# Attention plus gated MLP on one core: the first 512 tokens in two pairs of tiles, the maxima written from ScalarE's DMA queue, output loads issued over three steps

## The chip, the core and the metric

The kernel runs on one core of one Trainium2 chip. A core has five engines with queues of their own: TensorE (PE, matmuls; PEld is its weight load), VectorE (DVE), ScalarE (ACT), GpSimd (POOL) and SyncE (SP, which here only issues DMAs). Matmul results go to PSUM, eight banks of 128 partitions x 512 floats; everything else lies in SBUF or, through DMAs, in device memory. The metric is device time in microseconds of one execution, the median over the runs.

## The reference

```python
# x: 2048 tokens x 512; 32 heads of 16; gMLP with 896 + 896 features
def _A_ref(x, wqkv, wo):                      # attention
    q, k, v = ...(x @ wqkv)...                # (B, H, S, 16) each
    p = softmax(einsum("bhqd,bhkd->bhqk", q, k) * 16 ** -0.5)
    return (p @ v).merged_heads @ wo
def _B_ref(x, w_in, w_sp, b_sp, w_out):       # mixer
    z = gelu(x @ w_in)
    z1, z2 = z[..., :896], layernorm(z[..., 896:])
    g = einsum("ts,bsf->btf", w_sp, z2) + b_sp[None, :, None]
    return (z1 * g) @ w_out

x = A_x
xn = layernorm(x)
return x + _A_ref(xn, A_wqkv, A_wo) + _B_ref(xn, B_w_in, B_w_sp, B_b_sp, B_w_out)
```

## The kernel before

**Precision.** Matmuls take operands of type fp32r. Where full precision is wanted an operand is kept as two parts, high and low: the high part is a copy into fp32r, the low part is the difference between the value and the high part. A product is then three matmuls into one PSUM bank: high by high, low by high, high by low (`mm3`, lines 161 to 164). `split` makes both parts from PSUM, the high one on ACT, the low one on DVE. The pair of buffers `hilo` exists three times.

**Layout.** 16 tiles of 128 tokens make 4 groups of 512. Heads come in 16 pairs `p`; m (0 to 3) counts blocks of 128 columns of Q or K, which serve four pairs each. The operands of a pair's scores lie in the stacks `qst` and `kst`, two of each, used in turn; they are written from scratch tensors in device memory (`qscr`, `kscr`) by `load_stacks`.

**Prologue** (from line 816 on). Everything is emitted in the order written by hand, and every engine runs its own instructions in that order. `load_x(g)` loads 4 token tiles in two DMAs of 512 KB; `norm_x` is the layer norm (statistics on DVE, scale and shift on ACT) in two parts of two tiles; it is a generator, and each `next` emits a further piece. `turn_x(g)` transposes a group, 16 transposes of 128x128 through PSUM, for one block of 128 features after the other, into `xnT`, split into high and low; one PSUM buffer of the tag `s`, of which there are three, serves each of the four blocks. Weights come by `begin` (DMA into a buffer for raw values and, in the prologue, a second DMA of the same values on POOL's queue straight into the high part) and `end` (low part, on DVE in the prologue; elsewhere POOL copies the high part and subtracts). Then for each group: `qk_group` makes Q and K of m = 0 (24 matmuls), `v_tile` four V tiles (12 matmuls each), and after two of these the next group is transposed. The four V weight blocks are parked in the second pair of stacks. Stores of `xnT` go by POOL's queue until the prologue ends.

**Main loop** (from line 947 on). It runs over halves of steps; a pair of halves handles three key tiles. `b` counts key tiles and begins below zero, since the row maxima run 27 steps (`LEAD`) ahead of the scores. In each half the maxima's matmuls (`max_mm`, tile `mx`, line 630), DVE's reduction (`max_red`, line 638), the scores (tile `st`, line 903), ACT's exponential (`exp`, into `pf`) and, in even halves, the product with V (`pv`, tile `o`, line 877) are emitted. `st` and `mx` share the three PSUM buffers of the tag `s`. PSUM banks d and o take the accumulators.

When the sixteenth step of a maximum group is reduced, `max_fin` forms the negated maxima of 512 queries in two parts, transposes them into `ms` (line 657), writes them to `mscr` and reads them back into two extra rows for each head of `qst`. `later(k, ...)` emits a DMA k halves later on SP's queue; here the write comes one half later and the four reads two halves later.

All other matmul work (the rest of Q and K, both MLP projections, the spatial product, the output products) are generators in `queue`, drawn in odd halves up to a credit in nanoseconds of PE. While b is below 0 the credit is 2600 in every half, even ones included; afterwards it comes from what is left to do. `mlp_out` makes the MLP's output tiles: for each it loads two pieces `hp` of the hidden product and the token tile `xr` one tile ahead, all three at once.

**The planner's estimates.** `gps(us)` adds a duration to `pool[0]`, an estimate of when POOL will have finished; `pool_done` lets a generator wait until the estimated clock has reached it. `load` holds estimates for ACT and DVE. These decide where instructions are put, not when they run.

Of the kernel before, what the change touches and what calls it, by code (L numbers as in the profile page):

```python
# [8 lines left out]
F32 = mybir.dt.float32  # L9
# [7 lines left out]
P = 128  # L17
# [22 lines left out]
def fused_block(ctx, tc, x, wqkv, wo, w_in, w_spT, b_sp, w_out, out):  # L40
# [59 lines left out]
    def move(dst, src):  # L100
        nc.sync.dma_start(raw(dst), raw(src))
# [23 lines left out]
    def later(k, fn, *args):  # L125
        late.append((now[0] + k, fn, args))

    def flush():
        due = [l for l in late if l[0] <= now[0]]
        late[:] = [l for l in late if l[0] > now[0]]  # L130
        for _, fn, args in due:
            fn(*args)
# [35 lines left out]
    def begin(nm, src, n, blocks=1, t=None, early=None):  # L168


        t = piece(nm) if t is None else t
        rw = t512(nm + "r") if early == "t" else big.tile([P, 512], F32, tag="raw", name=nm + "r", bufs=3)
        dst, hi = rw[:, :n], t[:, 0, :n]
        if blocks > 1:
            src = src.rearrange("(c p) f -> p c f", p=P)
            dst, hi = (v.rearrange("p (c f) -> p c f", c=blocks) for v in (dst, hi))
        move(dst, src)
        if early:
            nc.gpsimd.dma_start(hi, src)
        return t, rw, n  # L180

    def end(loaded, early=False):
        t, rw, n = loaded
        if early:
            nc.vector.tensor_sub(t[:, 1, :n], rw[:, :n], t[:, 0, :n].bitcast(F32))
        else:
            gps(0.6).tensor_copy(t[:, 0, :n], rw[:, :n])  # L187
            gps(1.3).tensor_sub(t[:, 1, :n], rw[:, :n], t[:, 0, :n].bitcast(F32))
        return t
# [33 lines left out]
    def load_x(g):  # L223
        xt = [at.tile([P, 2, D], F32, tag="pf", name=f"x{g}_{i}", bufs=PF) for i in (0, 2)]
        for i in range(len(xt)):
            k = 4 // len(xt)
            t = 4 * g + k * i
            rows = x[t * P:(t + k) * P, :]
            move(xt[i], rows if k == 1 else rows.rearrange("(a p) d -> p a d", p=P))
            for j in range(k):  # L230
                xs[g, k * i + j] = xt[i] if k == 1 else xt[i][:, j, :]

    def norm_x(g, parts=1):


        mv = sm.tile([P, 4, 2], F32, tag="mv", name=f"mv{g}", bufs=2)
        rs = sm.tile([P, 2, 4], F32, tag="rs", name=f"rs{g}", bufs=2)
        k = 4 // parts
        for a in range(parts):
            tiles = range(a * k, (a + 1) * k)  # L240
            sl = slice(a * k, (a + 1) * k)
            for i in tiles:
                st = sm.tile([P, 6], F32, tag="bst", name=f"bst{g}_{i}", bufs=4)
                nc.vector.bn_stats(st, xs[g, i])
                nc.vector.bn_aggr(mv[:, i, :], st)
            yield
            nc.scalar.activation(rs[:, 0, sl], mv[:, sl, 1], AF.Sqrt, bias=epst)
            nc.vector.reciprocal(rs[:, 0, sl], rs[:, 0, sl])
            nc.vector.scalar_tensor_tensor(rs[:, 1, sl], mv[:, sl, 0], -1.0, rs[:, 0, sl], ALU.mult, ALU.mult)
            for i in tiles:  # L250
                if i % 4 == 2:
                    yield
                nc.scalar.activation(xs[g, i], xs[g, i], AF.Identity, bias=rs[:, 1, i:i + 1], scale=rs[:, 0, i:i + 1])

    def turn_x(g):
        for c in range(ND):
            pt = spsum(f"xT{g}_{c}")[:, 0, :]
            for i in range(4):
                nc.tensor.transpose(pt[:, i * P:(i + 1) * P], xs[g, i][:, c * P:(c + 1) * P], ident)
            t = piece(f"xnT{g}_{c}")  # L260
            split(t[:, 0, :], t[:, 1, :], pt, 512)
            store(xscr[g][c], t)
            xnT[g, c] = t

    def fetch_xnT(g, k=0):

# [64 lines left out]
                yield from qk_group(m, g, [wq[m, a] for a in range(2)])  # L331


    def v_tile(t, ws):
        acc = dpsum(f"v{t}", "do"[t % 2])
        sl = slice((t % 4) * P, (t % 4 + 1) * P)
        for c in range(ND):
            xt = xnT[t // 4, c]
            mm3(acc, xt[:, 0, sl], xt[:, 1, sl], ws[c][:, 0, :], ws[c][:, 1, :], c == 0, c == ND - 1)
        act(vhead[:, t, :, :DH], acc.rearrange("p (h d) -> p h d", d=DH), AF.Copy, 512)  # L340
# [224 lines left out]
    def mlp_out():  # L565
        def load(t):
            hp = []
            for i, n in enumerate((4, 3)):
                h = piece(f"hp{t}_{i}")
                move(h[:, :, :n * P].rearrange("p a (f q) -> p a f q", q=P), hscr[t // 4][:, :, t % 4, 4 * i:4 * i + n, :])  # L570
                hp.append(h)
            xt = t512(f"xr{t}")
            move(xt, x[t * P:(t + 1) * P, :])
            return hp, xt

        nxt = load(0)
        yield -3
        for t in range(NT):
            hp, xt = nxt
            if t + 1 < NT:  # L580
                nxt = load(t + 1)
            if t == NT - 1:
# [12 lines left out]
            yield 0  # L595
# [14 lines left out]


    NSTEP = NP * 64
    mstep = {}
    mmax = {}

# [24 lines left out]
    def max_fin(i):  # L640
# [15 lines left out]
        ms = at.tile([P, 32], F32, tag="ms", name=f"ms{g}", bufs=2)  # L656
        nc.vector.transpose(ms, mrow.bitcast(F32))
        load["D"] += 0.6
        later(1, move, mscr[g % 4].rearrange("b k x -> (b k) x"), ms)
        for j in range(2):  # L660
            for a in range(2):
                row = 64 * j + KS + a
# [150 lines left out]

    engines = {mybir.EngineType.PE, mybir.EngineType.Activation, mybir.EngineType.DVE, mybir.EngineType.Pool, mybir.EngineType.SP}
    with tc.manual_schedule(engines=engines):
        load_x(0)
        w0 = [begin(*qk_weights(0, a), early="t") for a in range(2)]
        load_x(1)
        ones = big.tile([P, 512], F32, tag="raw", name="ones", bufs=3)
        nc.vector.memset(ones[0:32, 0:P], 1.0)  # L820
        wv = []
        for c in range(ND):
            t = (qst, kst)[c // 2][1].rearrange("p (b a f) -> p b a f", b=2, a=2)[:, c % 2]
            wv.append(begin(f"wv{c}", wqkv[c * P:(c + 1) * P, 2 * D:3 * D], 512, t=t, early="rt"[c % 2]))
        nc.gpsimd.dma_start(cscr.rearrange("o (a b) -> (o a) b", b=P), ones[0:16, 0:P])
        nc.gpsimd.memset(vhead[:, :, :, DH:], 1.0)
        nc.gpsimd.memset(vall[:, NT * H * (DH + 1):], 0.0)
        run(norm_x(0, 2))
        load_x(2)
        w0 = [end(l, True) for l in w0]  # L830
        turn_x(0)
        load_x(3)
        init_rows(0)
        wv = [end(l, True) for l in wv]
        norm = norm_x(1, 2)
        for g in range(NG):
            for y in qk_group(0, g, w0, ("d", "o")):
# [105 lines left out]
        for half in range(-2 * LEAD // 3, 2 * (N // 3 + 4)):  # L943
# [109 lines left out]
```

## Time and profile before

| | |
|---|---|
| median of 3 runs | 1964.72 us (1963.83 to 1965.18) |
| profiled execution | 1965.23 us, of which the span of the trace 1963.1 us |
| mean granted TensorE clock | 0.997 |
| DMA | 294.20 MB, mean 150 GB/s |
| SP's DMA queue waiting for `ms` of DVE | 210.8 us in 58 waits |
| SP's DMA queue waiting for the landing of `mscr` | 81.1 us in 48 waits |

The page gives, for each engine, its busy time and share of the span; PE's ends are modelled, so a busy PE is not necessarily PE at its peak rate. The costliest groups of instructions follow, with the mean of one and the idle time of the engine before them:

```profile
L638 DVE TENSOR_REDUCE mm<-mx 128x2 f32<-128x1024 f32 x1024 | 1221.5, 1222 | 501.3 <-PE mx L630 497.2
L57 ACT ACTIVATE pf<-st 128x1024 f32<-128x1024 f32 x1024 | 1028.7, 1025 | 621.9 <-PE st L903 597.2
L877 PE MATMUL o<-pf,vall 128*32 128x512 f32 (+1 forms) x5120 | 511.0, 513 | 0.0
```

In a line of the timeline the first number is the start in us from the start of the span, the second how long the merged instructions took from first start to last end, then engine, line, operation, output and inputs, shape and count; in brackets stands how long the engine had been idle before it and who released it. Line 57 is a helper through which most of ACT's work goes, line 101 the helper of SP's DMAs, so such lines are told apart by their tiles.

### The profile page before, as it was taken

Reading aid. Unit: us, or ns where it says so; the run is one execution under the profiler, and the core shown is the slowest. Engines: PE = TensorE matmul, PEld = TensorE weight load, DVE = VectorE, ACT = ScalarE, POOL = GpSimd, SP = SyncE. Lnnn points to the kernel's source line nnn. Section 1 sums busy time; section 2 is a strip of 40 time slices with the busy share of each in tenths; the row PEclk is TensorE's granted clock in tenths of the full one; section 3 lists DMA queues with packets and bytes.
Section 4 is the critical chain, followed back from the end, with each engine's and each line's share of the span. In section 5 each row is a group of like instructions: output and inputs, shape, how many; then the busy total and the mean of one; then the engine's idle time right before and its main releaser. Section 6 shows DMA issues by size and latency. Waiting matters only on the chain.

```text
span 1963.1 us, 32545 instructions
## 1 busy us (share of the span) xinstructions
PE 1933.9 (99%) x12544; PEld 1047.0 (53%) x12544; DVE 1372.9 (70%) x1562; ACT 1231.7 (63%) x1402; POOL 720.9 (37%) x787
## 2 busy tenths in 40 slices
PE   7999999999999999999999999999999999999998
PEld 6765555555555555555555555555555555555543
DVE  5256777777777677777777777777777777777872
ACT  4336778888777665656666665665566655556664
POOL 2234368789776931026122531017112300002100
PEclk9999999999999999999999999999999999999999
DMA  9586444363535645365545744346364645355323
GB/s 327 204 292 200 139 107 122 108 176 111 154 117 159 187 123 140 91 162 159 151 138 154 211 129 125 108 126 204 105 163 135 176 142 145 106 152 154 105 73 113
DMA packets 234195, 294.20 MB, mean 150 GB/s; under 512 B 34536, under 2 KB 134520, under 8 KB 231160
## 3 DMA queue, kind: packets, MB, share of 16 engines
q1 hardware_dynamic: 229816, 282.08, 49.4%
q0 software_dynamic: 4224, 10.04, 1.4%
q8 instruction: 99, 1.62, 0.3%
q14 instruction: 56, 0.46, 0.1%
HBM read 190.09 MB, written 101.97 MB: 149 GB/s over the span
## 4 chain that ended last, share of the span: by engine, by line
PE 91%; DVE 3%; POOL 2%; DMA 2%; ACT 1%; issue 1%; SPq 0%; DVEq 0%; POOLq 0%; ACTq 0%
PE o L877 23%; PE mx L630 15%; PE st L903 15%; PE sp L162 7%; PE sp L164 5%; PE sp L163 5%; PE mo L162 2%; PE z1p L162 2%; PE qk L162 1%; DVE mm L638 1%; PE mo L163 1%; PE mo L164 1%; PE z2p L162 1%; PE z1p L164 1%; PE z1p L163 1%; PE qk L163 1%
## 5 line engine op out<-in xcount | busy, mean ns | idle before, releaser
L638 DVE TENSOR_REDUCE mm<-mx 128x2 f32<-128x1024 f32 x1024 | 1221.5, 1222 | 501.3 <-PE mx L630 497.2
L57 ACT ACTIVATE pf<-st 128x1024 f32<-128x1024 f32 x1024 | 1028.7, 1025 | 621.9 <-PE st L903 597.2
L877 PE MATMUL o<-pf,vall 128*32 128x512 f32 (+1 forms) x5120 | 511.0, 513 | 0.0
L630 PE MATMUL mx<-kst,qst 48*128 48x512 f32 x2048 | 446.9, 434 | 3.1 <-DVE mm L638 2.0
L903 PE MATMUL st<-qst,kst 50*128 50x512 f32 x2048 | 445.6, 432 | 1.5 <-DVE mm L638 1.4
L630 PEld LDWEIGHTS mx<-kst,qst 48*128 48x128 f32 x2048 | 192.0, 185 | 268.7 <-ACT pf L57 168.6
L903 PEld LDWEIGHTS st<-qst,kst 50*128 50x128 f32 x2048 | 193.3, 185 | 164.0 <-issue 85.7
L877 PEld LDWEIGHTS o<-pf,vall 128*32 128x32 f32 x5120 | 131.4, 109 | 233.7 <-issue 211.7
L162 PE MATMUL sp<-wsp,zs 128*128 128x512 f32 x448 | 193.8, 433 | 0.3 <-DVE z1i L549 0.2
L556 POOL TENSOR_TENSOR z1i<-z1i,hhl 128x512 f32<-128x512 f32 x28 | 36.0, 1286 | 425.9 <-DVE z1i L549 422.4
L164 PE MATMUL sp<-wsp,zs 128*128 128x512 f32 x448 | 175.9, 393 | 0.0
L163 PE MATMUL sp<-wsp,zs 128*128 128x512 f32 x448 | 175.9, 393 | 0.0
L162 PEld LDWEIGHTS sp<-wsp,zs 128*128 128x128 f32 x448 | 83.9, 187 | 68.9 <-issue 52.1
L164 PEld LDWEIGHTS sp<-wsp,zs 128*128 128x128 f32 x448 | 84.1, 188 | 19.3
L163 PEld LDWEIGHTS sp<-wsp,zs 128*128 128x128 f32 x448 | 84.4, 188 | 12.2
L187 POOL CAST wo<-wo0r 128x512 fp32r<-128x512 f32 x1 | 0.6, 611 | 191.4 <-DMA wo0r<-in_wo 191.4
L310 POOL TENSOR_TENSOR qkhl<-qr,qkhl 128x512 fp32r<-128x512 f32 x24 | 30.9, 1289 | 78.9 <-ACT qkhl L57 78.8
L162 PE MATMUL z2p<-w,xt 128*128 128x448 f32 x128 | 51.3, 401 | 0.0
L162 PE MATMUL mo<-wout,hp 128*128 128x512 f32 x112 | 48.5, 433 | 0.6 <-DVE xr L593 0.4
L691 POOL TENSOR_TENSOR ob<-ob 128x512 f32<-128x512 f32 (+1 forms) x16 | 20.6, 1288 | 77.0 <-DMA ob<-rscr 54.5
L164 PE MATMUL z2p<-w,xt 128*128 128x448 f32 x128 | 46.9, 366 | 0.0
L163 PE MATMUL z2p<-w,xt 128*128 128x448 f32 x128 | 46.8, 365 | 0.0
(378 smaller groups left out, 1974.8 us busy)
## 6 DMA issues: line engine op xcount, KB each, us to landing
zs<-z2scr SPq DMA_DIRECT2D x112, 512.0 KB
escr<-e SPq DMA_DIRECT2D x60, 256.0 KB
hscr<-hhl SPq DMA_DIRECT2D x28, 512.0 KB
qst<-qscr SPq DMA_DIRECT2D x30, 384.0 KB
kst<-kscr SPq DMA_DIRECT2D x30, 384.0 KB
xscr<-xnT POOLq DMA_DIRECT2D x16, 512.0 KB, 6.0
qscr<-qkhl SPq DMA_DIRECT2D x16, 512.0 KB
kscr<-qkhl SPq DMA_DIRECT2D x16, 512.0 KB
```

The lines of the kernel that those rows point to most:

```text
L57: return nc.scalar.activation(out, in_, func, **kw)
L162: nc.tensor.matmul(acc, lh, rh, start=first, stop=False)
L163: nc.tensor.matmul(acc, ll, rh, start=False, stop=False)
L164: nc.tensor.matmul(acc, lh, rl, start=False, stop=last)
L187: gps(0.6).tensor_copy(t[:, 0, :n], rw[:, :n])
L310: gps(1.3).tensor_sub(hl[:, 1, :], src, hl[:, 0, :].bitcast(F32))
L556: gps(1.3).tensor_add(z1, z1, hl[:, 1, :].bitcast(F32))
L630: nc.tensor.matmul(acc[:, j, :], qst[p % 2][rows, tt * P:(tt + 1) * P], kst[p % 2][rows, kc * 512:(kc + 1) * 512], start=True, stop=True)
L638: dve(1024).tensor_reduce(mmax[i // 16][:, :, t, kc], mstep.pop(i), AX.X, ALU.max)
L691: gps(1.3).tensor_mul(both[rows, 0, :], both[rows, 0, :], both[rows, 2, :])
L877: nc.tensor.matmul(acc[cols:cols + VW, a:a + w], vpack(kt - 1 + r, 2 * p + j), pf[:, j * 512 + a:j * 512 + a + w], start=(kt == 1 and a == ...
L903: nc.tensor.matmul(st[:, j, :], kst[p % 2][rows, kt * P:(kt + 1) * P], qst[p % 2][rows, c * 512:(c + 1) * 512], start=True, stop=True)
```

## The change

It has five parts.

1. *Prologue.* The second DMA of each early weight block on POOL's queue is gone. Of the V weights, blocks 0 and 3 get their high part on ACT and their low part on DVE, blocks 1 and 2 both parts on POOL, as do the two Q/K blocks. x of group 0 comes in four DMAs of one tile, with the first V block between them; V's weights are loaded ahead of those of Q and K. Tiles 0 and 1 are normalised, transposed and split by themselves (`turn_x(0, 0, 2)`); V tiles 0 to 3 come first, the other two token tiles being transposed in the middle of V tile 1, and Q and K of group 0 after them. `turn_x` writes its transposes into both banks of three PSUM buffers, all before the first split. Group 1 is transposed inside the first group of Q and K, groups 2 and 3 where they were. An early Sqrt is put first on ACT.
2. `pool[0]` is set back to -1000 when the prologue's first part is emitted.
3. The write of `ms` to `mscr` is issued by ACT's queue, one half after `max_fin`, behind the first exponential of that half.
4. In `mlp_out` the three loads for the next tile are emitted one, two and three halves later (for the first tile, at once).
5. At b = 0, in a half in which no product with V was emitted, the credit is 2600 too, so that projection steps are also drawn in the even half.

```diff
+    def soon(k, fn, *args):
+        fn(*args)
...
         move(dst, src)
-        if early:
-            nc.gpsimd.dma_start(hi, src)
         return t, rw, n
 
-    def end(loaded, early=False):
+    def end(loaded, low=None, high=False):
         t, rw, n = loaded
-        if early:
-            nc.vector.tensor_sub(t[:, 1, :n], rw[:, :n], t[:, 0, :n].bitcast(F32))
+        if high:
+            low.tensor_sub(t[:, 1, :n], rw[:, :n], t[:, 0, :n].bitcast(F32))
+        elif low:
+            nc.scalar.activation(t[:, 0, :n], rw[:, :n], AF.Copy)
+            low.tensor_sub(t[:, 1, :n], rw[:, :n], t[:, 0, :n].bitcast(F32))
         else:
             gps(0.6).tensor_copy(t[:, 0, :n], rw[:, :n])
             gps(1.3).tensor_sub(t[:, 1, :n], rw[:, :n], t[:, 0, :n].bitcast(F32))
...
     def load_x(g):
...
+            if g == 0:
+                for j in range(k):
+                    move(xt[i][:, j, :], x[(t + j) * P:(t + j + 1) * P, :])
+                    yield
+            else:
+                move(xt[i], x[t * P:(t + k) * P, :].rearrange("(a p) d -> p a d", p=P))
...
-    def turn_x(g):
+    def turn_x(g, lo=0, hi=4):
+
+        tiles = [spsum(f"xT{g}_{lo}_{c}") for c in range(3)]
+        sl = slice(lo * P, hi * P)
         for c in range(ND):
-            pt = spsum(f"xT{g}_{c}")[:, 0, :]
-            for i in range(4):
-                nc.tensor.transpose(pt[:, i * P:(i + 1) * P], xs[g, i][:, c * P:(c + 1) * P], ident)
-            t = piece(f"xnT{g}_{c}")
-            split(t[:, 0, :], t[:, 1, :], pt, 512)
-            store(xscr[g][c], t)
-            xnT[g, c] = t
+            for i in range(lo, hi):
+                nc.tensor.transpose(tiles[c % 3][:, c // 3, i * P:(i + 1) * P], xs[g, i][:, c * P:(c + 1) * P], ident)
+        for c in range(ND):
+            if lo == 0:
+                xnT[g, c] = piece(f"xnT{g}_{c}")
+            t = xnT[g, c]
+            split(t[:, 0, sl], t[:, 1, sl], tiles[c % 3][:, c // 3, sl], (hi - lo) * P)
+            if hi == 4:
+                store(xscr[g][c], t)
...
-    def v_tile(t, ws):
+    def v_tile(t, ws, mid=None):
...
         for c in range(ND):
+            if c == 2 and mid:
+                mid(t + 1)
...
-                move(h[...], hscr[t // 4][...])
+                (later if t else soon)(i + 1, move, h[...], hscr[t // 4][...])
...
-            move(xt, x[t * P:(t + 1) * P, :])
+            (later if t else soon)(3, move, xt, x[t * P:(t + 1) * P, :])
...
-        later(1, move, mscr[g % 4].rearrange("b k x -> (b k) x"), ms)
+        behind.append((now[0] + 1, mscr[g % 4].rearrange("b k x -> (b k) x"), ms))
...
-        load_x(0)
-        w0 = [begin(*qk_weights(0, a), early="t") for a in range(2)]
-        load_x(1)
+        nc.scalar.activation(mhalf, epst, AF.Sqrt)
+        nc.vector.memset(mhalf, -0.5)
+        first = load_x(0)
+        next(first)
+        next(first)
         wv = []
         for c in range(ND):
             wv.append(begin(f"wv{c}", ...))
+            if c == 0:
+                run(first)
+        w0 = [begin(*qk_weights(0, a), early="t") for a in range(2)]
+        run(load_x(1))
+        run(load_x(2))
...
+        norm = norm_x(0, 2)
+        next(norm)
+        nc.scalar.activation(wv[0][0][:, 0, :], wv[0][1], AF.Copy)
+        next(norm)
+        wv[0] = end(wv[0], nc.vector, True)
+        next(norm)
+        wv[1:3] = [end(l) for l in wv[1:3]]
+        turn_x(0, 0, 2)
+        wv[3] = end(wv[3], nc.vector)
         nc.gpsimd.dma_start(cscr.rearrange("o (a b) -> (o a) b", b=P), ones[0:16, 0:P])
         nc.gpsimd.memset(vhead[:, :, :, DH:], 1.0)
         nc.gpsimd.memset(vall[:, NT * H * (DH + 1):], 0.0)
-        run(norm_x(0, 2))
-        load_x(2)
-        w0 = [end(l, True) for l in w0]
-        turn_x(0)
-        load_x(3)
+        w0 = [end(l) for l in w0]
+        run(norm)
+        v_tile(0, wv)
+        v_tile(1, wv, lambda t: turn_x(0, 2, 4))
+        norm1 = norm_x(1, 2)
+        next(norm1)
+        v_tile(2, wv)
+        next(norm1)
+        next(norm1)
+        v_tile(3, wv)
+        run(norm1)
+        run(load_x(3))
         init_rows(0)
-        wv = [end(l, True) for l in wv]
-        norm = norm_x(1, 2)
+        pool[0] = -1000.0
         for g in range(NG):
+            once = True
             for y in qk_group(0, g, w0, ("d", "o")):
-                if y == 0 and g == 0:
-                    next(norm, 0)
+                if y == 0 and once and g < 2:
+                    once = False
+                    if g == 0:
+                        turn_x(1)
+                        norm = norm_x(2)
+                    else:
+                        next(norm)
...
-            for t in range(4 * g, 4 * g + 4):
+            for t in range(4 * g, 4 * g + 4) if g else ():
...
+            before = done
...
+            while behind and behind[0][0] <= half:
+                nc.scalar.dma_start(*behind.pop(0)[1:])
...
-            if b < 0:
+            if b < 0 or b == 0 and done == before:
                 credit = 2600
```

More of the change, by code (lines that the diff above doesn't have):

```diff
@@ L172, in begin @@
         rw = t512(nm + "r") if early == "t" else big.tile([P, 512], F32, tag="raw", name=nm + "r", bufs=3)
-        dst, hi = rw[:, :n], t[:, 0, :n]
+        dst = rw[:, :n]
         if blocks > 1:
             src = src.rearrange("(c p) f -> p c f", p=P)
-            dst, hi = (v.rearrange("p (c f) -> p c f", c=blocks) for v in (dst, hi))
+            dst = dst.rearrange("p (c f) -> p c f", c=blocks)
         move(dst, src)
-        if early:
-            nc.gpsimd.dma_start(hi, src)
         return t, rw, n
-    def end(loaded, early=False):
+    def end(loaded, low=None, high=False):
         t, rw, n = loaded
-        if early:
-            nc.vector.tensor_sub(t[:, 1, :n], rw[:, :n], t[:, 0, :n].bitcast(F32))
+        if high:
[3 more added lines that the diff above has]
+            low.tensor_sub(t[:, 1, :n], rw[:, :n], t[:, 0, :n].bitcast(F32))
         else:
@@ L225, in load_x @@
         for i in range(len(xt)):
-            k = 4 // len(xt)
+            k = 2
             t = 4 * g + k * i
-            rows = x[t * P:(t + k) * P, :]
-            move(xt[i], rows if k == 1 else rows.rearrange("(a p) d -> p a d", p=P))
             for j in range(k):
-                xs[g, k * i + j] = xt[i] if k == 1 else xt[i][:, j, :]
+                xs[g, k * i + j] = xt[i][:, j, :]
+            if g == 0:
[4 more added lines that the diff above has]
+                move(xt[i], x[t * P:(t + k) * P, :].rearrange("(a p) d -> p a d", p=P))
     def norm_x(g, parts=1):
@@ L240, in norm_x @@
             tiles = range(a * k, (a + 1) * k)
+            if a:
+                yield
             sl = slice(a * k, (a + 1) * k)
@@ L569, in load @@
                 h = piece(f"hp{t}_{i}")
-                move(h[:, :, :n * P].rearrange("p a (f q) -> p a f q", q=P), hscr[t // 4][:, :, t % 4, 4 * i:4 * i + n, :])
+                (later if t else soon)(i + 1, move, h[:, :, :n * P].rearrange("p a (f q) -> p a f q", q=P), hscr[t // 4][:, :, t % 4, 4 * i:4 * i + n, :])
                 hp.append(h)
             xt = t512(f"xr{t}")
-            move(xt, x[t * P:(t + 1) * P, :])
+            (later if t else soon)(3, move, xt, x[t * P:(t + 1) * P, :])
             return hp, xt
@@ L612, in fused_block @@
     NSTEP = NP * 64
+    behind = []
     mstep = {}
@@ L815, in fused_block @@
     with tc.manual_schedule(engines=engines):
-        load_x(0)
-        w0 = [begin(*qk_weights(0, a), early="t") for a in range(2)]
-        load_x(1)
-        ones = big.tile([P, 512], F32, tag="raw", name="ones", bufs=3)
-        nc.vector.memset(ones[0:32, 0:P], 1.0)
+        nc.scalar.activation(mhalf, epst, AF.Sqrt)
[3 more added lines that the diff above has]
+        next(first)
         wv = []
@@ L824, in fused_block @@
             wv.append(begin(f"wv{c}", wqkv[c * P:(c + 1) * P, 2 * D:3 * D], 512, t=t, early="rt"[c % 2]))
+            if c == 0:
[3 more added lines that the diff above has]
+        run(load_x(2))
+        ones = big.tile([P, 512], F32, tag="raw", name="ones", bufs=3)
+        nc.vector.memset(ones[0:32, 0:P], 1.0)
+        norm = norm_x(0, 2)
[7 more added lines that the diff above has]
+        wv[3] = end(wv[3], nc.vector)
         nc.gpsimd.dma_start(cscr.rearrange("o (a b) -> (o a) b", b=P), ones[0:16, 0:P])
```

## The prediction

> **What bounds the kernel now.** I read the page first, then busy time by stages, then who TensorE (PE) waited for, then the timeline at the few places where it waited.
>
> ```profile
> PE 1933.9 (99%) x12544; PEld 1047.0 (53%) x12544; DVE 1372.9 (70%) x1562; ACT 1231.7 (63%) x1402; POOL 720.9 (37%) x787
> ...
> PEclk9999999999999999999999999999999999999999
> ```
>
> ```profile
> 0.00:24.00 24.00, 14.48 (x60) 11.47 (x61) 15.43 (x39) 10.81 (x18) 10.21 (x23) 1.00 1.04 342
> 24.00:80.00 56.00, 54.00 (x261) 44.58 (x260) 18.66 (x39) 24.36 (x43) 10.17 (x16) 1.00 0.72 270
> 80.00:143.90 63.90, 61.48 (x269) 43.14 (x267) 32.71 (x32) 20.05 (x33) 25.42 (x22) 1.00 0.71 249
> 143.90:152.00 8.10, 7.01 (x35) 3.66 (x34) 4.71 (x4) 5.34 (x7) 1.35 (x2) 0.79 0.71 262
> ...
> 300.00:500.00 200.00, 197.93 (x1313) 107.59 (x1312) 150.94 (x181) 162.91 (x204) 170.95 (x218) 1.00 0.47 134
> 500.00:1900.00 1400.00, 1398.28 (x9258) 732.20 (x9261) 1021.14 (x1119) 868.79 (x937) 429.14 (x426) 1.00 0.50 142
> 1900.00:1964.00 64.00, 52.73 (x380) 23.45 (x372) 22.23 (x28) 32.04 (x36) 0.92 (x2) 0.94 0.26 87
> ```
>
> The columns are length, then busy time of PE, its weight loads, DVE, ACT and POOL, then granted clock, DMA share and GB/s. PE is the bound: from 152 to 1900 us it is idle for about 4 us in all. Nothing there can give much unless it removes matmuls, and the change removes none. What can be had lies before 152 us: 9.5 idle in the first 24, 2.0 in 24 to 80, 2.4 in 80 to 143.9, 1.1 and a clock of 0.79 after that. The tail after 1900 is not touched.
>
> ```profile
> 10.91 3.04 PE L259 MATMUL xT<-ident,x 128*128 128x128 f32 x13 [0.23 <-ACT x L253]
> ...
> 13.60 0.63 PE L162 MATMUL qk<-xnT,wqk 128*128 128x512 f32 x1
> ...
> 25.80 1.20 PE L259 MATMUL xT<-ident,x 128*128 128x128 f32 x9 [0.28 <-ACT x L253]
> ...
> 27.54 0.66 PE L259 MATMUL xT<-ident,x 128*128 128x128 f32 x4 [0.54 <-DVE xnT L159]
> ...
> 33.50 0.39 PE L162 MATMUL qk<-xnT,wqk 128*128 128x512 f32 x1
> ```
>
> The first projection starts at 13.60, since it takes all four token tiles; transposing the next 512 tokens stops in the middle, waiting for the split that frees its PSUM buffer. At 33.50 the first group of Q and K, four V tiles and the next transposes are done: my milestone for the prologue.
>
> ```profile
> 136.18 0.63 ACT L57 ACTIVATE qkhl<-qr 128x512 fp32r<-128x512 f32 x1 [7.16 <-DMA kscr<-qkhl]
> ...
> 137.35 0.50 PE L162 MATMUL qk<-xnT__1182,wqk 128*128 128x512 f32 x1 [1.55 <-ACT qr L57]
> ```
>
> ```profile
> 146.00 0.50 PE L630 MATMUL mx<-kst,qst 48*128 48x512 f32 x2 [1.08 <-DVE mm L638]
> ...
> 148.38 0.63 PE L162 MATMUL qk<-xnT__1184,wqk 128*128 128x512 f32 x1
> ```
>
> ```profile
> 143.66:147.07 3.41, 2.33 (x15) 1.06 (x13) 1.75 (x2) 2.72 (x5) 0.30 (x1) 1.00 0.97 357
> 147.07:150.48 3.41, 3.41 (x10) 2.28 (x12) 1.83 (x2) 1.48 (x2) 1.29 (x1) 0.50 0.33 125
> ```
>
> A store that lands late holds the high/low buffer, ACT sits behind it for 7.16 us, and PE then loses 1.55. At the first step with scores PE waits 1.08 for a reduction, and right after it the clock is at half for 3.41 us.
>
> **The change part by part.** *Prologue.* The second copies of six weight blocks (6 x 256 KB on POOL's queue) go; their high parts are made on ACT (two) and POOL (four), so 1.5 MB less is moved in a stretch with a DMA share of 1.04. When do the new inputs land? I take the bytes that the old run had moved: 232 GB/s over the first 7.13 us is 1.65 MB, then 337 GB/s. In the new order on SP's queue wv1 is complete at 1.57 MB, wv2 at 1.84, wv3 at 2.1: about 6.8, 7.7 and 8.5 us. Ten issues of 0.48 us on SP (row of x) do not hold this up. POOL needs 0.61 (its CAST row) and 1.29 (its 128x512 subtraction) for each block: wv1 done at 8.7, wv2 at 10.6, then 1.9 us for memsets and a DMA, and the two Q/K blocks (2 x 1.9) at about 16.3.
>
> The first pair of tiles was normalised at 8.53 (two activations from 7.01 for 1.52); x arrives now in single tiles, a little earlier, but ACT's 0.6 copy of wv0 is put ahead of it: I take 8.3. Eight transposes at 0.2 (13 in 2.64 above) and one 256-wide split, about 0.4 on ACT and 0.35 on DVE (rows of 0.60 and 0.69 for 512), let V start at 10.2. ACT then makes wv3's high part, DVE its low part: 11.9; V reaches it after nine matmuls of 0.228 (steps of the rows from 23.67 on), 12.3. No wait. The second pair is normalised at about 13.8, behind tile 0 and half of tile 1; no wait either. From 10.2: 48 V matmuls (10.9), 24 of Q and K (5.5), 8 transposes (1.0), 16 for the next group (2.4, without the stop): 30.0. Add a slow start: the first qk matmul stands 0.47 before the next, later ones 0.23, so PE ran at half rate until 13.95; V would run there for between none and 1.7 us lost, taken at 0.9. So 30.9 against 33.5: **-2.6**. The stops of 0.76 us (0.28 and 0.54 at the first, much the same at the next two) go also for the last two groups, whose sixteen transposes no longer reuse a buffer: **-1.5**. Together -4.1; bounds -1 (transfers 2 us later than I count, cold start in full) and -5.5. Q/K of the first group comes some 10 us later, but the maxima wait for the last group's stacks, whose order is unchanged; V of that group, 11 us long, still covers their landing. x(3) now waits for the second pair's transposes (15 us) on SP, ahead of the Q stores that come after 24: hidden; its tiles are used after 45.
>
> *GpSimd's estimate set back* only keeps the planner's clock of POOL where it was (-1000 then too), so nothing is delayed by the six new POOL jobs. The early Sqrt moves nothing: the table load already stands at 0.72. Both 0.
>
> *The step b = 0.* Four projection steps (12 matmuls, 2.7 us of PE) are put into the half in which PE waited 1.08, and about two more into the next. The work is only drawn forward, so the wait goes: -1.1; and if the half clock came of that thin stretch, 8 or so matmuls at 0.43 instead of 0.23 go as well: -1.7. I take **-2.8**, bounds 0 and -2.8. By "TensorE: Matmul & The Clock Gate" of the Trainium skill (What's actually happening) the array falls to half rate after an idle window of about 3.4 us; the window before the drop has 2.33 us of busy PE in 3.41, so the trace does not agree, and by the rule alone the sum would keep 1.7 us (a rival below).
>
> *Maxima by ACT's queue.*
>
> ```profile
> L101 SPq DMA_DIRECT2D mscr<-ms x64: 314/326/627, 117.0 to 1907.9; - x64
> ```
>
> ```profile
> 1012.75 1.02 ACT L57 ACTIVATE pf<-st 128x1024 f32<-128x1024 f32 x1 [0.63 <-PE st L903]
> 1015.67 2.06 ACT L57 ACTIVATE pf<-st 128x1024 f32<-128x1024 f32 x2 [1.90 <-PE st L903]
> ```
>
> 64 issues leave SP, where the queue stood 210.8 us for DVE's `ms` (58 times), and come to ACT behind the exponential of the odd half. No trace shows this issue on ACT; the nearest row is SP's, 0.33 us. Will it wait? The DVE transpose ended at 1012.31, before that exponential even starts; its neighbours are alike (0.3 to 0.9 us before, in nearly all). Behind it stand the next exponentials, for which ACT idles 1.90 here, 0.78 at the tightest I looked at (299.90): 0.33 is covered. If it were not, 64 x 0.33 = 21 us. For SP, the reads of `mscr` still wait for a landing, now about 1.4 us later, but rows of qst are needed some 20 us on. Stores queued behind the `ms` wait go earlier; that can ease the 7.16 us block at 136: **-0.8**, half of PE's 1.55, bounds 0 and -1.55. In the steady part, bounds -2 (300 to 500 is 2.1 short of full) and +2.6 (8 issues of 0.33 uncovered there, where ACT is busy 162.91 of 200): 0.
>
> *Output loads one, two and three halves later.* Tiles of that stage start 11.7 to 15.4 us apart, halves are about 2.7 us: the last needed half of h comes 5.4 us in, 3 us to land, before the next tile. x's tile is read only at the end. 0, bounds 0 and +1 (no PE wait on `hp` exists to be saved).
>
> Sum: -4.1 - 2.8 - 0.8 = -7.7, on the profiled 1965.23 (span 1963.1 and 2.1 around it) 1957.5; the median of the runs is 0.5 lower: **1957.0**.
>
> **The rivals.** *The transfers of 115 to 144 us take the prologue's gain back*: DMA share 0.96 to 1.05 there, a store landing 8.6 us after issue. If the stores rather than PE pace that stage, the 4.1 and 0.8 are lost and 2.8 stays: 1961.9. Against it: PE idles only 2.4 of 64 us, so the pace is PE's. *The extra steps at b = 0 fill the three high/low buffers* and ACT stands behind a landing with exponentials queued: about 7 us (the 7.16 row) less the 2.7 of drawn-forward work, +4.5: 1961.5. Against: the blocks just before 144 are 0.8 us. *The clock drops all the same*: 1.7 kept, 1958.7. *Slower: ACT pays for the issues.* If one takes 1.7 us on ACT (the longest SP issue of an output load, 1.696), 0.5 us sticks out of a gap of 1.2 at some 32 of 64 places and the whole of it where ACT is packed: +16, net 1973. It decides from 1.4 us an issue, when 64 x 0.18 eats gain and margin. Against: every SP row of this transfer is under 0.63. *The change does not do what it says*: V waits for POOL's wv2 or for late x and the prologue gains 1: 1960.
>
> **How the numbers follow.** Forecast 0.48 (own range 1953 to 1960); clock drops anyway 0.10; prologue gains little 0.10; transfers take it back 0.13; buffers at b = 0 0.06; ACT pays 0.13. What this measurement can tell is about 0.2%, 3.9 us: the first three are faster (0.68), the next two within it (0.19), the last slower (0.13). Range 1951 to 1966: the low end takes the bounds of prologue, steady part and the 1.55; the high end covers the cases of no change and leaves out most of the slow one.
>
> **What would show it.** V's first matmul near 10 us; the second group of Q and K starting near 31; no stop inside a group's transposes; no half clock near 143; ACT's issue of `mscr` short, and the exponentials behind it no later than their scores; no PE wait on `hp`. It is wrong if the milestone gains but the first score does not come as much earlier, or if PE from 152 to 1900 shows new waits on ACT.

## The result, and the profile after

The change made the kernel slower: 1969.18 us (1967.28 to 1971.7, 17 runs) against 1965.18 us before (1963.24 to 1968.49, 17 runs) on the same chip, a ratio of 1.0021 with a 95% interval of 1.0014 to 1.0028. The forecast was 1957.0, with a range of 1951 to 1966. The profiled execution took 1968.24 us, its span 1966.1; before these were 1965.23 and 1963.1. So the profiled execution lies 10.7 us above the sum's 1957.5.

The page's busy times and the table by stages (length, busy time of PE, its weight loads, DVE, ACT and POOL, granted clock, DMA share, GB/s) of the kernel after:

```profile
PE 1935.7 (98%) x12544; PEld 1046.9 (53%) x12544; DVE 1373.2 (70%) x1565; ACT 1233.6 (63%) x1409; POOL 721.8 (37%) x785
```

```profile
0.00:24.00 24.00, 14.97 (x55) 11.82 (x56) 9.73 (x31) 10.19 (x21) 13.11 (x24) 1.00 0.78 267
24.00:80.00 56.00, 55.63 (x271) 46.43 (x270) 21.73 (x48) 26.58 (x47) 10.90 (x18) 1.00 0.76 281
80.00:142.50 62.50, 60.35 (x264) 42.19 (x262) 32.72 (x32) 19.81 (x32) 25.38 (x22) 1.00 0.71 247
142.50:153.80 11.30, 7.86 (x37) 5.33 (x36) 3.58 (x3) 5.25 (x8) 2.71 (x3) 1.00 0.99 340
...
500.00:1900.00 1400.00, 1397.37 (x9251) 729.69 (x9251) 1022.43 (x1119) 868.90 (x936) 420.39 (x416) 1.00 0.50 141
```

Two stages tell the story. From 24 to 80 us PE is idle for 0.37 us where it was 2.0, so the stops are gone. From 142.5 to 153.8, the first steps with scores, PE is busy for 7.86 of 11.30, at a full clock: 3.4 us of new waits stand just where the forecast had 2.8 us to gain. From 500 to 1900 us PE is idle for 2.6 us instead of 1.7, too little for the table to show where.

The prologue, PE's timeline of the kernel after (start, duration, engine, line, operation, tiles, shape, count, idle before):

```profile
11.23 0.79 PE L165 MATMUL v<-qst,xnT 128*128 128x512 f32 x1 [0.47 <-ACT xnT L57]
...
16.98 0.63 PE L166 MATMUL v<-qst,xnT 128*128 128x512 f32 x1
17.40 0.44 PE L167 MATMUL v<-qst,xnT 128*128 128x512 f32 x1
17.68 0.40 PE L165 MATMUL v<-qst,xnT 128*128 128x512 f32 x1
...
28.84 1.91 PE L271 MATMUL xT<-ident,x 128*128 128x128 f32 x16
33.31 0.39 PE L165 MATMUL qk<-xnT,wqk 128*128 128x512 f32 x1
```

V starts at 11.23 (10.2 was forecast), and its steps are 0.43 apart until 17.40, 0.23 after that: half rate, though the window's clock column says 1.00. Fourteen steps take the 6.17 us from 11.23 to 17.40; at 0.228 they would take 3.2. So 3.0 are lost, where the forecast allowed 0.9. The sixteen transposes of a group run without a stop. The milestone comes at 33.31, hardly earlier than 33.50; the first matmul of the maxima, behind two more groups without stops, at 86.61 where it was 87.76.

The step b = 0, PE and ACT in the timeline of the kernel after:

```profile
143.08 1.94 ACT L57 ACTIVATE pf<-st 128x1024 f32<-128x1024 f32 x2 [0.53 <-PE st L949]
144.91 0.60 ACT L57 ACTIVATE qr<-qk 128x512 f32<-128x512 f32 x1
145.56 0.50 PE L165 MATMUL qk<-xnT__1193,wqk 128*128 128x512 f32 x1 [2.07 <-ACT qr L57]
...
150.25 0.59 ACT L57 ACTIVATE qr<-qk 128x512 f32<-128x512 f32 x1
150.89 0.50 PE L165 MATMUL qk<-xnT__1193,wqk 128*128 128x512 f32 x1 [1.37 <-ACT qr L57]
```

A projection group ends, and the next one, drawn forward into this half, accumulates in the same bank. It can't begin before ACT has copied the bank out (`qr<-qk`), and that copy stands behind two exponentials. PE waits 2.07 us, and 1.37 at the next group, whose copy stands behind one.

PE's waits after (line, what it waits for, us in all, times, longest); below them two waits of the kernel before; then, of the kernel after, the issue of the maxima (ns shortest, median, longest) and SP's queue:

```profile
PE qk L165 <- ACT qr L57: 4.7, 3, 2.1
PE st L949 <- DVE mm L656: 2.9, 9, 0.6
PE mx L648 <- DVE mm L656: 0.9, 1, 0.9
```

```profile
PE mx L630 <- DVE mm L638: 2.0, 2, 1.1
PE qk L162 <- ACT qr L57: 1.5, 1, 1.5
```

```profile
L1019 ACTq DMA_DIRECT2D mscr<-ms x64: 326/326/357, 115.9 to 1911.4; - x64
```

```profile
SPq L101 <- DMA mscr<-ms: 276.0, 57, 16.2
```

The wait for `qr` was 1.5 us in one place before and is 4.7 in three. Of the two waits of `mx` for a reduction the one of 1.08, which the step b = 0 was to take away, is gone, and in this execution no spell of half clock follows: what was to go did go, and the new waits are larger. An issue costs ACT 0.33 us, as the row of SP had it. SP's queue is no freer: it waits 276.0 us for the landing of `mscr`, where it had stood 210.8 for `ms` and 81.1 for the landing.

### The profile page after: what moved, and what is told of

Its sections match the earlier page's. It is cut to its first block, busy times and chain, and to the rows that moved or that the text cites. A ratio compares the mean times of both kernels' runs of the same rounds, so it can differ in the third digit from the quotient of the medians.

```text
span 1966.1 us, 32533 instructions
## 1 busy us (share of the span) xinstructions
PE 1935.7 (98%) x12544; PEld 1046.9 (53%) x12544; DVE 1373.2 (70%) x1565; ACT 1233.6 (63%) x1409; POOL 721.8 (37%) x785
## 3 DMA queue, kind: packets, MB, share of 16 engines
q8 instruction: 99, 1.62, 0.3%
## 4 chain that ended last, share of the span: by engine, by line
PE 88%; DVE 3%; issue 1%; ACT 1%; POOL 0%; DVEq 0%; ACTq 0%; POOLq 0%
PE o L923 23%; PE st L949 15%; PE mx L648 15%; PE sp L165 7%; PE sp L167 5%; PE sp L166 5%; PE mo L165 2%; PE z2p L165 2%; PE z1p L165 2%; DVE mm L656 2%; PE mo L167 1%; PE mo L166 1%; PE z2p L167 1%; PE z2p L166 1%; PE z1p L167 1%; PE z1p L166 1%
```

## The experiments

Each kernel is compared with the kernel before, in five rounds, by the median of its runs on the same chip.

**One part alone.** *The prologue* (parts 1 and 2 of the change, without the other three):

> The kernel before with the prologue of the change alone. Theory A (the loss comes of the steps drawn at b = 0, the prologue's small gain stays): 1 to 2 us faster than before, the first maximum matmul about 1.2 us earlier, as in the trace of the whole change. Rival B (the loss comes of the maxima on ScalarE's queue): the same here. Rival C (the prologue itself sets the later stages wrong, by other estimates or by transfers): 2 to 4 us slower.

Measured: 1961.88 us against 1965.93, ratio 0.9981 (0.9972 to 0.9989), so 4.05 us less. *The step b = 0* on the kernel before:

```diff
+            before = done
...
-            if b < 0:
+            if b < 0 or b == 0 and done == before:
                 credit = 2600
```

> The kernel before with the credit at b = 0 alone. Theory A: 2 to 5 us slower, from waits between 230 and 720 us, where a projection's steps now fall on other halves than before. Rival B and C: 0 to 3 us faster, by the wait and the half clock at 146 us.

Measured: 1970.24 us, ratio 1.0028 (1.0017 to 1.0039). It is slower by itself, without the new prologue and without ACT's issues, and its waits of PE are those of the kernel after:

```profile
PE qk L162 <- ACT qr L57: 4.6, 3, 2.1
PE st L903 <- DVE mm L638: 2.9, 9, 0.6
```

*The maxima by ACT's queue* on the kernel before:

```diff
-        later(1, move, mscr[g % 4].rearrange("b k x -> (b k) x"), ms)
+        behind.append((now[0] + 1, mscr[g % 4].rearrange("b k x -> (b k) x"), ms))
...
+            while behind and behind[0][0] <= half:
+                nc.scalar.dma_start(*behind.pop(0)[1:])
```

> The kernel before with the write of the maxima on ScalarE's queue alone. Theory A and C: within 1 us of before. Rival B: 2 to 5 us slower, with exponentials that start later behind the issue.

Measured: 1964.97 us, ratio 0.9996 (0.9988 to 1.0005): no effect that can be told. *The output loads* on the kernel before, with the diff's `later if t else soon` at the three loads:

> The kernel before with the output loads spread alone. All theories: within 1 us of before; a loss here would be one that none of them has.

Measured: 1964.71 us, ratio 0.9996 (0.9987 to 1.0005). So the loss is part 5's, and the other parts don't produce it.

**Taken out of the whole.** The kernel after with `if b < 0:` as before:

> The whole change without the credit at b = 0. Theory A: 4 to 5 us faster than before (the prologue alone gave 4.0 of medians, maxima and loads about 0.5 each within their noise); no pair of halves over 6 us before 190 us. If parts of the change work against each other: only 0 to 2 us faster.

Measured: 1961.85 us against 1965.58, ratio 0.9979 (0.9970 to 0.9988). The step b = 0 costs the whole change 1969.18 - 1961.85 = 7.3 us; with each kernel taken against the kernel before on its own chip (+4.0 and -3.7), 7.7. By itself it cost 4.3 (interval 3.3 to 7.7). The two waits are 3.4; the question is what else it does.

**Another bank.** In every half below -2 a group accumulates by turns in banks d and o; from half -2 on it has d alone. This kernel is the one after, but the group that starts in half 0 accumulates in o, which has no other use at that time:

```diff
-            acc = dpsum(f"qk{m}_{a}_{g}", tags[a % len(tags)], ND)
+            acc = dpsum(f"qk{m}_{a}_{g}", "o" if now[0] == 0 and m else tags[a % len(tags)], ND)
```

> The whole change, but the group of projections that starts in the even half of b = 0 accumulates in PSUM bank o, which nothing else uses yet, instead of d, where it has to wait until ScalarE has copied the group before out, behind two exponentials. Theory A1 (part of the loss is this wait): PE waits of 2.07 and 1.37 us on ScalarE's copy go or shrink below 0.5 each, 2 to 3 us faster than the whole change, later stages as before. Rival A2 (all of the loss is the later phase of the projection steps): within 1 us of the whole change.

Measured: 1964.02 us against 1965.58, ratio 0.9992 (0.9983 to 1.0001), 5.2 us less than after (5.6 with each taken against the kernel before on its own chip). PE's timeline of this kernel, the same steps as above, and the row of the table by stages:

```profile
142.73 0.40 PE L949 MATMUL st<-qst,kst 50*128 50x512 f32 x2
143.06 0.50 PE L165 MATMUL qk<-xnT__1193,wqk 128*128 128x512 f32 x1
...
146.95 0.50 PE L165 MATMUL qk<-xnT__1193,wqk 128*128 128x512 f32 x1
...
149.94 0.50 PE L949 MATMUL st<-qst,kst 50*128 50x512 f32 x2
```

```profile
142.50:153.80 11.30, 11.30 (x60) 6.91 (x57) 6.23 (x6) 8.45 (x12) 2.68 (x3) 1.00 1.02 352
```

No line has a bracket, and PE is busy for all of the 11.30 us: it waits nowhere. The first pair of halves with scores runs from its first matmul `st` to that of the next pair. Here are these two in `before`, then in `max_only`:

```profile
143.94 0.50 PE L903 MATMUL st<-qst,kst 50*128 50x512 f32 x2
...
149.79 0.79 PE L903 MATMUL st<-qst,kst 50*128 50x512 f32 x2
```

```profile
143.77 0.50 PE L904 MATMUL st<-qst,kst 50*128 50x512 f32 x2
...
148.38 0.50 PE L904 MATMUL st<-qst,kst 50*128 50x512 f32 x2
```

The pair in all of these kernels (duration in us / projection matmuls in it):

```
before 5.86/6   max_only 4.61/6   ahead 4.61/6
b0_only 12.83/24   after 11.33/24   after_bank 7.79/24
```

In `before` and `b0_only` a spell of half clock falls into this pair, worth 1.25 and 1.5 us; the other four run at full clock and can be compared. Eighteen more matmuls at 0.228 are 4.1 us, so 4.61 would become 8.71 if nothing else changed. In the other bank it is 7.79, a gain of 0.9, about the wait of 1.08 that goes; in the one bank it is 11.33, a loss of 2.6, since two waits of 3.44 come in its place. Taking the waits away therefore confirms them as the first cause. But 1964.02 is still above 1961.85, the kernel that doesn't draw forward at all.

**Where the rest goes.** I lined up the traces by PE's work: the times at which each has done the same sum of matmul steps, as us ahead (-) or behind (+) of the kernel before. Own computation; the columns are about 89, 167, 252, 498 and 956 us and shortly before the end (1950). Where two kernels have their projections at different places, a lag is good to about half a microsecond, since it hangs on what a step is taken to count:

```
              89     167     252     498     956     end
after       -1.16   -1.00   +0.41   +1.12   +3.30   +3.05
after_bank  -1.97   -4.87   -3.61   -2.97   -0.33   -0.15
pro_only    -2.44   -2.77   -2.92   -3.28   -3.38   -2.93
max_only    +0.26   -1.72   -1.74   -2.11   -1.85   -1.47
```

Between 89 and 167 the kernel with the other bank wins 2.9 us, as much as the forecast had for this step. But `max_only`, whose matmuls stand as those of `before`, wins 2.0 there as well, most of it because no spell of half clock falls into its first pair; only the other 0.9 is the step's. Then `after_bank` gives back 4.5 us over the next 800, and the kernel after loses as much (4.3); the prologue alone and `max_only` give back nothing. Drawing six projection steps forward at b = 0 leaves the later steps four to six places ahead until about 440 us and two to six until about 950 (12 to 18 and 6 to 18 more matmuls done at the start of a pair, counted in the traces). The rival to "places" is that something else in the change does it. Two kernels tell these apart from both sides: `ahead` has no change at b = 0 but runs four to eight steps ahead from about 200 to 440 us, on places that are not all those of the kernel after; `payback` keeps the step at b = 0 with the other bank, and has its six steps paid back by half 25.

```diff
+                credit = min(credit + (355 if 3 <= b <= 33 else 0) + 3 * (max(todo...
```

> The whole change without the credit at b = 0, but with 355 more credit in each of the eleven pairs of halves from b = 3 to b = 33, so that the projection steps run as far ahead as with it, without anything drawn at b = 0. Rival A2 (running ahead puts the layer norm's statistics and the maxima's last reductions on the same pairs): 2 to 4 us slower than the kernel without that credit, with the losses near 250 and 445 us. Theory A1 alone: within 1 us of it.

Measured: 1964.41 us against 1965.58, ratio 0.9993 (0.9984 to 1.0002), 2.6 us above the kernel that it is made from. Its lag goes from -4.02 at 167 to -1.16 at 956: much the same giving back, with nothing changed at b = 0.

```diff
+                credit = min(credit - (310 if 3 <= b <= 33 else 0) + 3 * (max(todo...
```

> The whole change with bank o for the group at b = 0, and with 310 less credit in each of the eleven pairs of halves from b = 3 to b = 33, so that from half 25 on every projection step stands in the half in which it stands without the credit at b = 0 (but for two halves out of the rest). Theory A2 (the later loss comes of where the steps stand): the gain of about 3 us at b = 0 stays to the end; no loss at 250 or 445 us; 1 to 3 us faster than without the credit at b = 0, 3 to 5 faster than with it and bank o. Rival A3 (drawing work forward costs by itself what it gains, wherever the steps then stand): as with bank o alone, about 1964.

Measured: 1961.44 us against 1965.71, ratio 0.9973 (0.9963 to 0.9983), 2.6 us below `after_bank`. Its lag is -2.74 at 167 and -2.88 at 956. The intervals of these pairs touch or just overlap (0.9983 bounds both here), so 2.6 is not exact; the lags carry the finding. But 1961.44 is also no better than 1961.85 without the step: done right in both respects, drawing forward at b = 0 gains nothing that can be told. The forecast of 1 to 3 us below that kernel is missed, as the "gain of about 3 us" that it started from was for the most part the spell in the profile of `before`.

**What a place costs.** One of the places, 248 us, in the timeline of the kernel after, DVE and PE:

```profile
245.74 0.21 DVE L675 STREAM_TRANSPOSE ms<-mrow 128x32 f32<-128x32 f32 x1
245.87 1.11 DVE L393 BATCH_NORM_STATS2 zst<-z 128x6 f32<-128x448 f32 x2
247.02 0.21 DVE L394 BATCH_NORM_AGGREGATE zmv<-zst 128x2 f32<-128x12 f32 x1
247.14 3.43 DVE L656 TENSOR_REDUCE mm<-mx 128x2 f32<-128x1024 f32 x3
...
249.50 0.50 PE L949 MATMUL st<-qst,kst 50*128 50x512 f32 x2 [0.63 <-DVE mm L656]
```

Six steps ahead, the statistics of a layer norm fall into the pair in which DVE also finishes the maxima; together they take 2.35 us beside DVE's reductions, the reductions come late and PE waits for them. The next kernel is `after_bank` with these statistics held back by a half when they meet the end of the maxima:

```diff
+                while fins[0] == now[0]:
+                    yield
...
+        fins[0] = now[0]
```

> The whole change with bank o for the group at b = 0, and with the layer norm's statistics held back by a half where they would be emitted in the half of the maxima's last reductions. Theory A2a (the later loss is the collision of these two on DVE): the wait at 248 us (pair 19, 7.0 us long) goes, the loss between 230 and 460 us shrinks by 1 us or more, 1 to 2 us faster than with bank o alone. Rival (the loss is spread over other waits): the wait at 248 moves to another pair and the time stays within 0.5 us.

Measured: 1962.54 us against 1965.71, ratio 0.9984 (0.9975 to 0.9992). DVE in its timeline:

```profile
240.38 0.21 DVE L678 STREAM_TRANSPOSE ms<-mrow 128x32 f32<-128x32 f32 x1
240.75 2.36 DVE L659 TENSOR_REDUCE mm<-mx 128x2 f32<-128x1024 f32 x2
243.02 1.14 DVE L395 BATCH_NORM_STATS2 zst<-z 128x6 f32<-128x448 f32 x2
```

Two reductions now come between, and the following pair is shorter (own computation; pair 18 with DVE's other work in brackets / pair 19 / pair 55, us). Pair 18 holds twelve projection matmuls in `before` and `payback` and six in the other three, pairs 19 and 55 twelve in all five:

```
before       5.96 (0.93) / 5.91 / 6.29
after        4.65 (2.35) / 7.00 / 7.61
after_bank   4.64 (2.35) / 7.04 / 7.62
apart        4.64 (0.95) / 6.34 / 7.62
payback      5.96 (0.94) / 5.91 / 6.28
```

At this place the mechanism is shown: the lag gained there shrinks from 0.9 to 0.2. Of the 1.5 us between the two medians this accounts for 0.7, and the intervals overlap, so the rest is not proved. The place at 445 us (pair 55, where the z2 projections give way to those of z1) loses the same 1.3 us with and without this edit; 0.3 of it is only that a step of z1 takes 0.231 us and one of z2 0.206. The part from 700 to 950 us is spread out. What makes those two places dear was not isolated.

Another place shows that not every loss in these profiles comes of the places. Pair 87, at 611 us, has twelve projection matmuls in four kernels and takes 7.92 us in `after_bank`, 7.58 in `after`, 6.60 in `apart` and 6.61 in `b0_only`. In `after_bank` ACT waits for POOL's `z` and its exponentials come late; in `b0_only`, which has the same steps at the same places and holds nothing back, the same instruction does not wait (`after_bank`, then `b0_only`):

```profile
613.30 0.63 ACT L57 ACTIVATE z<-z 128x512 f32<-128x512 f32 x1 [1.03 <-POOL z L364]
```

```profile
617.50 0.65 ACT L57 ACTIVATE z<-z 128x512 f32<-128x512 f32 x1
```

So 1.3 us of the 4.5 that `after_bank` gives back stand there, and neither the places nor the statistics alone account for them. By the medians the drift costs 2.2 to 2.6 us.

**The half rate at the start.** `after_no_b0` with thirty transposes of the identity while PE waits for x, into a buffer that nobody reads:

```diff
+        warm = spsum("warm")
+        for _ in range(30):
+            nc.tensor.transpose(warm[:, 0, 0:P], ident, ident)
```

> The whole change without the credit at b = 0, with 30 transposes of the identity into an unused PSUM buffer while PE waits for the first tokens. Theory W (V runs at half clock from 11 to about 15 or 17 us because PE was idle before): the clock is full when V starts, 1.5 to 3 us faster than the same without them. Rival: the activity of small transposes does not open the clock, or they delay the first real one: within 0.5 us or slower.

Measured: 1958.98 us against 1965.58, ratio 0.9965 (0.9953 to 0.9978). PE's timeline:

```profile
1.35 5.86 PE L838 MATMUL warm<-ident 128*128 128x128 f32 x30 [1.35 <-POOL ident masks.py:199]
...
10.08 0.50 PE L165 MATMUL v<-qst,xnT 128*128 128x512 f32 x1 [0.47 <-ACT xnT L57]
...
11.11 0.40 PE L165 MATMUL v<-qst,xnT 128*128 128x512 f32 x1
11.34 0.40 PE L166 MATMUL v<-qst,xnT 128*128 128x512 f32 x1
```

V now runs at 0.23 a step from its third matmul on, and the 2.9 us between the medians (1961.85 and 1958.98) are what half rate cost V in the profile of `after_no_b0`, whose first fourteen steps take 6.12 us (10.04 to 16.16) instead of 3.2. Every run of this kernel (1958.23 to 1960.26) lies below every run of `after_no_b0` (1960.27 to 1966.14). The same with `payback`:

> The same with the 30 transposes of the identity before the first tokens arrive. If the two gains are independent: 2 to 3 us faster again, 1956 to 1958, the fastest of all.

Measured: 1958.79 us against 1965.71, ratio 0.9961 (0.9947 to 0.9974). The forecast of 1956 to 1958 is missed, and it can't be told from `warm`; both beat the kernel before by some 7 us and the kernel after by 10.

## Why the prediction was wrong

**The step that failed is *The step b = 0*.** It was taken at -2.8 with bounds 0 and -2.8, on the ground that "the work is only drawn forward". In the whole change it is +7.3 by the medians, +7.7 against each one's own kernel before. Counted from -2.8 that is 10.5 of the 12.2 us between the forecast (1957.0) and the result; the other parts came 1.2 short (-3.7 for -4.9), and the kernel before was itself 0.5 slower than the median from which the forecast was counted (1965.18 for 1964.72). Three things were missed.

1. *Where the drawn group accumulates.* I asked what the added matmuls wait for, and looked at the high/low buffers (a rival) but not at the accumulator. With one bank the next group needs ACT's copy, and at b = 0 ACT has exponentials for the first time. My rival on filled buffers had the right engine with the wrong resource, and put it 4.5 us above the forecast, where the run came out 12.2 above. The other bank gives back 1969.18 - 1964.02 = 5.2 us; the waits that the trace shows are 3.4 of it, and where the rest lies is open.
2. *Drawn-forward work moves all that comes after it.* I closed the account at the next half. The later places cost 1964.02 - 1961.85 = 2.2 us (2.6 by `ahead` and by `payback`). A shift of six steps puts at least one set of DVE's statistics against its last reductions.
3. *The half clock.* The 1.7 was put down to the thin stretch with the 1.08 wait. That stretch, a window of 3.41 us with PE busy for 2.33, stands in five profiles; half clock follows it in two of them (`before` at 147.07, `pro_only` at 144.56) and not in `max_only`, `ahead` and `after_no_b0`. So it does not decide by itself, and one profile's spell was counted as a loss of every run. Its size was off as well: with the spell the pair takes 5.86 us and without it 4.61, so the spell cost 1.25.

**The prologue** was right: -4.1 forecast, -4.05 measured by itself and -3.7 with the maxima and output loads. Its terms were less exact, so that the sum agrees so closely is in part luck. The stops went, as counted. The start at half rate was taken at 0.9 of "none to 1.7" and is 2.9 to 3.0 in `after_no_b0` and after, because V starts earlier than any projection did and the clock opens no earlier. V itself starts at 11.23 in the kernel after, 1.0 later than counted. In the profile of `pro_only` the clock opens at 14.85, eight steps after V's start, and the first matmul of the maxima comes 2.4 us earlier than before, not 4.1; the interval of the runs (-2.2 to -5.5) holds both. Two sums of the prediction don't come out: 0.28 and 0.54 make 0.82, not 0.76, and the bounds that it names for the low end of the range give 1952.9, not 1951. Neither bears on the miss.

**Maxima by ACT's queue**, -0.8: what it was to ease did not ease. The high/low split at 134.76 has still been held for 6.88 us (7.16 before), and PE's wait behind it is 1.27 for 1.55:

```profile
134.76 0.63 ACT L57 ACTIVATE qkhl<-qr 128x512 fp32r<-128x512 f32 x1 [6.88 <-DMA kscr<-qkhl]
135.93 0.50 PE L165 MATMUL qk<-xnT__1193,wqk 128*128 128x512 f32 x1 [1.27 <-ACT qr L57]
```

By itself -0.8 lies inside the interval measured for it, but so does no effect at all. The cost side, 0.33 an issue and hidden, was right, and with it the rival *ACT pays* is out.

**Output loads**, 0: right within the interval; the profile after has no PE wait on `hp`.

**The rivals.** The one on the slower side had the wrong mechanism (an issue would have had to take over 1.4 us), the transfers did not take the prologue's gain back (`pro_only`), and *clock drops all the same* holds in that spells come and go, but by no rule that I can show. The Trainium skill says in "TensorE: Matmul & The Clock Gate" (What's actually happening) that the rate falls after an idle window of about 3.4 us. No window was idle, and the trace shows falls all the same. Two neighbouring windows and the spell of `after_no_b0`, in the table's columns:

```profile
128.73:132.14 3.41, 3.23 (x15) 1.88 (x14) 2.33 (x2) 0.00 (x0) 0.00 (x0) 1.00 0.99 354
132.14:135.55 3.41, 1.97 (x8) 0.81 (x6) 1.12 (x2) 0.51 (x1) 0.00 (x0) 1.00 1.05 407
135.55:142.38 6.83, 6.17 (x16) 4.30 (x16) 0.12 (x1) 2.95 (x6) 3.82 (x3) 0.50 0.83 312
```

PE was busy for 1.97 of 3.41 us before this fall, and for 1.18 to 2.33 before the seven others seen between 19 and 152 us. But windows of 1.62 (after) and 1.79 (`after_bank`) were followed by none, so busy time by the profile's records does not decide it, and what does stays open.

## What to carry to other kernels

Before drawing matmuls forward, follow their accumulator: which bank, who empties it, and what that engine has queued at the new place. In a kernel whose steps are placed one by one, a shift at one point is a shift of everything behind it, so line up the two traces by work done and look for a slow drift, which no single wait will show. A spell of half clock seen in one profile is not a cost of the kernel until a second profile has it at the same place.

## What the hardware showed that was not expected

The clock of the first matmuls opened at another time in every execution: 13.95 us before, 14.09 to 17.48 in the ten others without added work. Those times and the spells of half clock of one execution lie on one grid of 3.41 us (before: 13.95, and 147.07 is 39 steps later), and the grid stands elsewhere in each. Own computation, the window on that grid before the opening and the one before it, with PE's busy time:

```
before       7.12 1.25    10.54 3.18   opens 13.95
pro_only     8.03 2.49    11.44 3.41   opens 14.85
after_no_b0  9.26 2.94    12.67 3.41   opens 16.09
after       10.65 2.94    14.07 3.41   opens 17.48
payback     10.07 2.94    13.49 3.41   opens 16.90
warm         -            2.82 3.41    opens  6.23
```

In all thirteen profiles the clock opened after the first window with PE busy for 3.18 us or more, and 2.94 was not enough. The Trainium skill (same page and section) has a window that runs freely and opens after a busy one, and here the trace agrees. So V's earlier start was partly wasted by where the grid happened to stand, and thirty small transposes ahead of x, which fill a whole window, opened it at 6.23 and 6.65 and were worth 2.9 us.
